# Decayed attention ahead of two MLPs: the carried states as one scan per unit, chunk innermost, with four input slots and a smaller descriptor scratch

## The chip, the cores and the metric

One core of a Trainium2 chip runs the whole program. Its engines are TensorE (PE, with weight loads shown apart as PEld), VectorE (DVE), ScalarE (ACT), GpSimd (POOL) and SyncE (SP, whose queue issues the transfers). The metric is the device time of one execution in microseconds (us); lower is better.

## The reference

```python
batch, n_heads, seq, head_dim = (4, 8, 576, 64)
scores = scale * np.matmul(q, k.transpose(0, 1, 3, 2))
gamma = 1.0 - 2.0 ** (-5.0 - np.arange(H, dtype=np.float32))
rel = pos[:, None] - pos[None, :]
Dmat = np.where(rel >= 0, gamma[:, None, None] ** rel[None, :, :], 0.0)
ret = scores * Dmat[None, :, :, :]
attn_out = np.matmul(ret, v)
...
x = np.ascontiguousarray(attn_out.transpose(0, 2, 1, 3)).reshape(B * S, H * D)
h = np.maximum(x @ w_in, 0.0)        # 2304 x 512 by 512 x 2048
x = h * h @ w_out
a = x @ w_a                          # 2304 x 512 by 512 x 1536
b = x @ w_b
return (a * b @ w_out).astype(np.float32)
```

Attention has no softmax: a score is multiplied by a power of its head's decay. The sum over earlier tokens can therefore be carried from chunk to chunk as a state of 64 x 64 values per head.

## The kernel before, in words

**Attention.** The 576 tokens of a sequence are cut into 9 chunks of 64 (`C = 64`). Two heads make a pair, one head on partitions 0 to 63 and the other on 64 to 127. For each of the 4 sequences there are 5 units: one for each pair with its first 7 chunks (`LONG = 7`; `first` is 0), and one with the last 2 chunks of all four pairs. A unit loads its q and k into a slot of `qkr` and its v and k into a slot of `vr` (both rings of 3 slots). ScalarE scales a copy of v into `tv` (line 613). TensorE then makes three groups of 64x64 products in full fp32: the scores, the states (`tv` against k, a new contribution per chunk) and, one unit later, the sums (masked scores against v, and carried states against q). VectorE masks the scores into `pt` (line 700), carries the states in `carry_states` (lines 721 and 722) and scales the sums into the activations `xt` (line 685). The carry is one copy for the first chunk and then one fused multiply and add per chunk, out = before x decay + new, on 64 columns each. The carried states lie in `sa`, chunk after chunk; the last one of a pair goes to `sp`, from where the unit of the last chunks takes it up.

**MLPs.** Weights arrive as 64-bit words in `wraw` (and, early on, in a part of `xt` that is still free); ScalarE and VectorE turn each tile of 128x512 into fp32 (lines 369 to 399) and split it into a high and a low part (lines 240 and 243, tile `w`). The activations are split the same way into `xb`. `up` and `down` are the first MLP's two products for the chunks of `FIRST`; the rest of the program follows later and reads its weights back from memory (`kept`, `parts`).

**Order.** All work is first recorded as steps with costs per engine, then `Plan.order` writes one order for each engine by due times and modelled costs. Each engine runs its rows strictly in that order. Attention's units are put between the MLP's chunks at a rate (`RATE`), after the first sequence's units have been placed ahead of everything. All large transfers stand in one queue, SP's, and a transfer into a slot waits there until the slot's last reader is done.

Of the kernel before, what the change touches and what calls it, by code (L numbers as in the profile page):

```python
# [11 lines left out]
F32 = mybir.dt.float32  # L12
# [5 lines left out]
ALU = mybir.AluOpType  # L18
PSUM = bass.MemoryType.PSUM

B, H, S, D = 4, 8, 576, 64
NT, DM, F1, F2 = 2304, 512, 2048, 1536
P = 128
NP = H // 2
# [3 lines left out]
LONG = 7  # L28
# [22 lines left out]

WF, WL, WE, RAWS = 4, 4, 2, 2
SLOTS = dict(
    g=2, r=2, gh=2, qkr=3, vr=3, tv=2, pt=2, sa=2, wraw=4, ys=4,
)

POOL_SLACK, POOL_BIAS = 1e9, 1e6
# [159 lines left out]
def tile_retention_two_mlps(  # L217
# [10 lines left out]
    nc = tc.nc  # L228
    eng = {"ACT": nc.scalar, "DVE": nc.vector, "POOL": nc.gpsimd}
    V, A, G, T = nc.vector, nc.scalar, nc.gpsimd, nc.tensor  # L230
    plan = Plan()

    def mm(o, l, r, start, stop):
        T.matmul(o, l, r, start=start, stop=stop, skip_group_check=True)  # L234
# [30 lines left out]
    def ring(pool_, tag, shape, dtype, n):  # L265
        rings[tag] = [[pool_.tile(shape, dtype, name=f"{tag}{i}") for i in range(n)], 0]

    def slot(tag):
        r = rings[tag]
        i = r[1] % len(r[0])  # L270
        r[1] += 1
        plan.renew((tag, i))
        return r[0][i], (tag, i)
# [12 lines left out]
    st = ExitStack()  # L286
    ap = st.enter_context(tc.tile_pool(name="attn", bufs=1, side="right"))
# [2 lines left out]
    ring(ap, "vr", [P, 2 * LONG * D], F32, SLOTS["vr"])  # L290
    ring(ap, "tv", [P, LONG * D], F32, SLOTS["tv"])
    ring(ap, "pt", [P, most * C], F32, SLOTS["pt"])
    ring(ap, "sa", [P, (LONG - 1) * D], F32, SLOTS["sa"])

    ring(ap, "ys", [P, 512], F32, SLOTS["ys"])
    ring(ap, "wraw", [P, 1024], U32, SLOTS["wraw"])
    vt = ap.tile([P, 3 * NP], F32, name="vt")
    gt = ap.tile([P, NP, C], F32, name="gt")
# [5 lines left out]
    mask = ap.tile([P, C], F32, name="mask")  # L304
    md = ap.tile([P, NP, C], F32, name="md")
    sp = [ap.tile([P, D], F32, name=f"sp{p}") for p in range(NP)]

    V.memset(mask, 1.0)
    first = ap.tile([P, 2], F32, name="first")
# [225 lines left out]
    def attention():  # L535
        turn = [0]

        def banks(b):

            sets = [(4, 5, 6)] if b else [(4, 5, 6), (0, 1, 2)]  # L540
            turn[0] += 1
            return [(bank[i], ("bank", i)) for i in sets[turn[0] % len(sets)]]

        for h in half:
# [3 lines left out]
                lambda _, h=h: G.affine_select(  # L548
                    out=mask[h], in_=mask[h], pattern=[[1, C]], compare_op=ALU.is_ge, fill=zero,
                    base=0, channel_multiplier=-1,  # L550
                ),
# [3 lines left out]
        def decays(p):  # L555
            plan.add(
                {"DVE": 230},
                lambda e: V.tensor_scalar(
                    out=md[:, p], in0=mask, scalar1=vt[:, p:p + 1], scalar2=None, op0=ALU.mult
                ),  # L560
                [("mask",), ("vt",)], [("md", p)],
            )

        class Unit:

# [12 lines left out]
            def load(self):  # L578
# [24 lines left out]
                if b == 0 and self.p is not None:  # L603
                    decays(self.p)
# [14 lines left out]
        def cell(i, n=C):  # L619
            return slice(i * n, i * n + n)  # L620

        def products(new, old):

            b = (new or old).b
            (s, ks), (st, kst), (x, kx) = banks(b)
            scores, states, sums = [], [], []

            if new:  # L630
                n = len(new.cells)
                for i in range(n):
                    for h in half:
                        scores.append((s[h, cell(i)], new.r[h, cell(n + i)], new.r[h, cell(i)], i == 0))
                for i in range(len(new.leave)):
                    for h in half:
                        states.append((st[h, cell(i)], new.v[h, cell(n + i)], new.tv[h, cell(i)], i == 0))
            if old:
                for i in range(len(old.cells)):
                    for k, h in enumerate(half):  # L640
                        sums.append((x[half[1 - k], cell(i)], old.v[h, cell(i)], old.pt[h, cell(i)], i == 0))
                for i, (q, j) in enumerate(old.cells):
                    if j:
                        for k, h in enumerate(half):
                            sums.append((x[half[1 - k], cell(i)], old.state[q, j][h], old.r[h, cell(i)], False))

            def f(gs):
                for k in range(0, max(map(len, gs)), 2):
                    for g in gs:
                        for o, l, r, first in g[k:k + 2]:  # L650
                            mm(o, l, r, first, True)

            def run(keys, *gs):
                rd = [k for r, _ in keys for k in r]
                wr = [w for _, w in keys]
                plan.add({"PE": 58 * max(map(len, gs)) + 330}, lambda e: f(gs), rd, wr)

            ksc, kstt = ([new.kr], ks) if new else None, ([new.kv, new.kt], kst) if new else None
            ksu = ([old.kr, old.kv, old.kp] + old.kstate, kx) if old else None

            if b and new and old:
                run([ksc, kstt, ksu], scores + states, sums)
            else:
                if new:
                    run([ksc], scores)
                if old:
                    run([ksu], sums)
                if new:
                    run([kstt], states)
            if old:  # L670
                weigh(old, x, kx)
            if new:
                mask_scores(new, s, ks)
                carry_states(new, st, kst)

        def weigh(u, x, kx):

            np_, per = len(u.pairs), u.last - u.first
            c0 = u.b * S + u.first * C
            x = x[:, :np_ * per * C].rearrange("p (q c n) -> p q c n", q=np_, n=C)  # L680
            ps = slice(u.pairs[0], u.pairs[-1] + 1)
            n = per * C
            plan.add(
                {"DVE": 1.042 * np_ * n + 145},
                lambda e: V.tensor_tensor(
                    out=xt[:, ps, c0:c0 + n].rearrange("p q (c n) -> p q c n", n=C),
                    in0=x,
                    in1=gt[:, ps].unsqueeze(2).to_broadcast([P, np_, per, C]), op=ALU.mult,
                ),
                [("gt",), kx], [w for q in u.pairs for w in tokens("xt", q, c0, n)],  # L690
                [m for k in lenders for m in plan.users.get(k, ())] if c0 + n > LENT else (),
            )

        def mask_scores(u, s, ks):
            np_, per, n = len(u.pairs), u.last - u.first, len(u.cells)
            ps = slice(u.pairs[0], u.pairs[-1] + 1)
            u.pt, u.kp = slot("pt")
            plan.add(
                {"DVE": 1.042 * n * C + 145},
                lambda e: V.tensor_tensor(  # L700
                    out=u.pt[:, :n * C].rearrange("p (q c n) -> p q c n", q=np_, n=C),
                    in0=s[:, :n * C].rearrange("p (q c n) -> p q c n", q=np_, n=C),
                    in1=md[:, ps].unsqueeze(2).to_broadcast([P, np_, per, C]), op=ALU.mult,
                ),
                [ks] + [("md", q) for q in u.pairs], [u.kp],
            )

        def carry_states(u, st, kst):

            sa, ksa = slot("sa")  # L710
            u.state = {(q, LONG): sp[q] for q in u.pairs}
            u.kstate = [ksa] + ([("sp", q) for q in u.pairs] if u.first else [])
            for i, (q, j) in enumerate(u.leave):
                o, ko = (sp[q], ("sp", q)) if j + 1 == LONG else (sa[:, cell(i, D)], ksa)
                u.state[q, j + 1] = o
                before, kb = u.state.get((q, j)), [ksa, ("sp", q)]
                far = vt[:, 2 * NP + q:2 * NP + q + 1]

                def carry(e, o=o, i=i, before=before, far=far):
                    if before is None:  # L720
                        return V.tensor_copy(o, st[:, cell(i, D)])
                    return V.scalar_tensor_tensor(
                        out=o, in0=before, scalar=far, in1=st[:, cell(i, D)], op0=ALU.mult, op1=ALU.add
                    )

                rd = [kst, ("vt",)]
                if before is not None:
                    rd.append(("sp", q) if j == LONG else ksa)
                plan.add({"DVE": 270 if j else 222}, carry, rd, [ko])
# [3 lines left out]
        for n, (b, p) in enumerate(units):  # L733
            new = Unit(b, p)
# [156 lines left out]
    xo = []  # L891
    tmp = []

    rings_a = ["qkr", "vr", "tv", "pt", "wraw", "vt", "gt", "mask", "md", "sp", "sa", "ys"]

    def mlps():
        prev = None
# [10 lines left out]
    def rest():  # L908
# [430 lines left out]
        for _ in downs:  # L1339
            pass  # L1340

    att = attention()
    while env["done"] < READY[0]:
        next(att)
# [86 lines left out]
```

## Time and profile before

| what | value |
|---|---|
| time, median of 3 runs | 854.11 us (851.86 to 855.42) |
| the profiled execution's own time | 854.09 us |
| its span, first to last instruction | 852.4 us |
| TensorE busy | 834.8 us (98%), 6540 matmuls |
| VectorE busy | 731.9 us (86%) |
| ScalarE busy | 565.9 us (66%) |
| mean granted TensorE clock | 0.998 of full speed |

A busy share is a mean over the program; what the change can move is read from the stretch in which attention runs. The trace shows each fp32 64x64 product as two matmul instructions, so its counts for attention are twice those of the program's order.

### The profile page before, as it was taken

The page shows a single profiled execution, that of the slowest core. Times are in us where ns is not written, and L with a number is a line of the kernel's source. Part 1 is how long each engine was busy: PE and PEld are TensorE (multiplying, and loading weights), DVE is VectorE, ACT ScalarE, POOL GpSimd, SP SyncE. Part 2 cuts the span into 40 slices and gives each one's busy share as a digit, 9 for nine tenths or more (in the row PEclk, how much of TensorE's full clock was granted, in tenths as well). Part 3 has the DMA queues.
Part 4 walks back from the last instruction along what each step waited for, and adds up shares of the span by engine and source line. Part 5 has one row for each costly group of instructions (what it writes and reads, how often), then busy time and mean ns, then how long its engine had stood idle before and what let it go on. Part 6 is the DMA issues. An engine that isn't in the chain of part 4 may idle for free.

```text
span 852.4 us, 17685 instructions
## 1 busy us (share of the span) xinstructions
PE 834.8 (98%) x6540; PEld 801.4 (94%) x6540; DVE 731.9 (86%) x1531; ACT 565.9 (66%) x1180; POOL 0.7 (0%) x6
## 2 busy tenths in 40 slices
PE   5899999999999999999999999999999999999998
PEld 5788888889999999999999999999999999999997
DVE  5999874878799999999899989999786789888885
ACT  4676562767888877978796565676556576556560
POOL 0000000000000000000000000000000000000000
PEclk9999999999999999999999999999999999999999
DMA  9865861379877668757847888755554455655432
GB/s 322 296 238 187 290 217 62 113 251 301 264 249 236 210 216 257 229 190 242 294 151 237 286 294 285 222 172 171 160 187 145 142 164 163 184 175 163 138 90 75
DMA packets 89734, 176.15 MB, mean 207 GB/s; under 512 B 9904, under 2 KB 34864, under 8 KB 89648
## 3 DMA queue, kind: packets, MB, share of 16 engines
q1 hardware_dynamic: 89504, 175.02, 63.7%
q8 instruction: 51, 0.84, 0.4%
q14 instruction: 35, 0.29, 0.1%
q10 hardware_dynamic: 144, 0.01, 0.0%
HBM read 134.75 MB, written 40.24 MB: 205 GB/s over the span
## 4 chain that ended last, share of the span: by engine, by line
PE 86%; DMA 6%; DVE 4%; ACT 3%; issue 1%; SPq 0%; ACTq 0%; DVEq 0%
PE bank L234 86%; DMA w<-kept 2%; DMA raw<-w 2%; DMA wraw<-w 1%; ACT w L240 1%; DMA vr<-vk 1%; DVE w L243 1%; DVE xt L246 1%; DMA vt<-vtab 0%; DVE wf L388 0%; ACT tv L613 0%; ACT xb L240 0%; DVE wf L399 0%; ACT wf L369 0%; ACT bank L240 0%
## 5 line engine op out<-in xcount | busy, mean ns | idle before, releaser
L234 PE MATMUL bank<-xo,w 128*128 128x384 f32 x1838 | 389.5, 335 | 0.9 <-ACT bank L240 0.7
L234 PEld LDWEIGHTS bank<-xo,w 128*128 128x128 f32 x1838 | 324.3, 188 | 3.1 <-ACT bank L240 2.4
L234 PE MATMUL bank<-xb,w 128*128 128x384 f32 (+2 forms) x1044 | 229.1, 347 | 1.1 <-ACT r L824 0.8
L240 ACT CAST w<-w 128x512 fp32r<-128x512 f32 (+1 forms) x316 | 156.6, 519 | 86.2 <-DMA w<-kept 69.4
L234 PEld LDWEIGHTS bank<-xb,w 128*128 128x128 f32 x1044 | 184.1, 188 | 13.3 <-ACT r L824 1.2
L243 DVE TENSOR_TENSOR w<-w 128x512 fp32r<-128x512 f32 (+1 forms) x316 | 170.9, 560 | 20.8 <-ACT w L240 19.1
L234 PE MATMUL bank<-gh,w 128*128 128x384 f32 (+2 forms) x750 | 171.9, 352 | 0.2
L234 PEld LDWEIGHTS bank<-gh,w 128*128 128x128 f32 x750 | 131.9, 188 | 12.4 <-DVE w L243 0.5
L234 PE MATMUL bank<-w,w 128*128 128x384 f32 x546 | 123.9, 334 | 0.1
L234 PEld LDWEIGHTS bank<-w,w 128*128 128x128 f32 x546 | 97.1, 188 | 0.5 <-DVE xt L246 0.4
L246 DVE TENSOR_TENSOR xt<-bank,xt 128x384 f32<-128x384 f32 x128 | 69.7, 552 | 8.4 <-PE bank L234 7.9
L240 ACT COPY bank<-bank 128x384 f32<-128x384 f32 x122 | 57.2, 469 | 16.5 <-PE bank L234 13.9
L234 PE MATMUL bank<-ghl,w 128*128 128x384 f32 x186 | 40.9, 334 | 0.0
L243 DVE TENSOR_TENSOR xo<-xt,xo 128x768 fp32r<-128x768 f32 x36 | 33.6, 951 | 1.9 <-ACT xo L240 1.9
L395 ACT ACTIVATE we<-raw 128x512 int32<-128x512 uint32 x48 | 31.9, 668 | 3.1 <-DVE wf L399 1.5
L240 ACT CAST xo<-xt 128x768 fp32r<-128x768 f32 x36 | 29.1, 831 | 6.0 <-issue 5.4
L234 PEld LDWEIGHTS bank<-ghl,w 128*128 128x128 f32 x186 | 33.0, 188 | 0.0
L243 DVE TENSOR_TENSOR gh<-g,gh 128x512 fp32r<-128x512 f32 (+2 forms) x40 | 24.5, 614 | 8.1 <-ACT g L827 6.8
L399 DVE CUSTOM_DVE_ANT_0 wf<-wf,we 128x1024 uint16<-128x1024 uint16 x45 | 30.7, 685 | 0.4
L613 ACT ACTIVATE tv<-vr,vt 128x448 f32<-128x448 f32 (+1 forms) x32 | 15.0, 500 | 21.5 <-DMA vr<-vk 19.7
L824 ACT ACTIVATE r<-bank 128x512 f32<-128x512 f32 (+1 forms) x30 | 16.5, 551 | 19.1 <-PE bank L234 18.9
L234 PE MATMUL bank<-tv,vr 64*64 64x64 f32 x512 | 20.5, 233 | 8.6 <-ACT tv L613 8.6
(241 smaller groups left out, 962.2 us busy)
## 6 DMA issues: line engine op xcount, KB each, us to landing
w<-kept SPq DMA_DIRECT2D x167, 256.0 KB, 3.7
raw<-w SPq DMA_DIRECT2D x48, 512.0 KB, 4.7
w<-kept SPq DMA_DIRECT2D x149, 128.0 KB, 3.0
kept<-wf SPq DMA_DIRECT2D x49, 256.0 KB, 4.2
w<-parts SPq DMA_DIRECT2D x24, 512.0 KB, 3.5
kept<-wl SPq DMA_DIRECT2D x36, 256.0 KB, 4.9
wraw<-w SPq DMA_DIRECT2D x16, 512.0 KB, 7.3
vr<-vk SPq DMA_DIRECT2D x16, 448.0 KB, 5.3
```

What stands on the lines that cost most here:

```text
L234: T.matmul(o, l, r, start=start, stop=stop, skip_group_check=True)
L240: return lambda e: A.copy(o(), i()) if e == "ACT" else eng[e].tensor_copy(o(), i())
L243: return lambda e: eng[e].tensor_sub(o(), a(), b())
L246: return lambda e: eng[e].tensor_add(o(), a(), b())
L395: lambda e: A.activation(like(rest), lo(), AF.Copy, scale=LO_ULPS), [kraw], [ke],
L399: lambda e: V._custom_dve(ADD32_U16LIMBS, out=w().bitcast(U16), in0=w().bitcast(U16), in1=rest.bitcast(U16)),
L613: lambda e, to=to, ti=ti, q=q: A.activation(self.tv[:, to], self.v[:, ti], AF.Copy, scale=vt[:, NP + q:NP + q + 1]),
L824: lambda e, o=o: A.activation(r[:, :n], o[:, :n], AF.Relu), [ko], [kr],
```

## The change

Carrying the seven chunks of a full unit is now one VectorE scan over 448 columns. For that the states of a unit are written with the chunk innermost: chunk i of the state goes to columns i, i + 7, i + 14 and so on of its PSUM bank. Along a row the scan computes value = factor x previous + new, and the factor tile `fade` holds the pair's decay everywhere but in each seventh column, where it is 0 and so starts anew. `fade` is set up by two memsets and one multiplication per pair. The carried states are then read by TensorE at a stride of 7 elements, and the last one is copied to `sp` by ScalarE. The units of the last chunks keep the old form. `qkr` and `vr` have 4 slots in place of 3, `sa` one more chunk, and the program's scratch for dynamic descriptors is set to 1024.

```diff
 SLOTS = dict(
-    g=2, r=2, gh=2, qkr=3, vr=3, tv=2, pt=2, sa=2, wraw=4, ys=4,
+    g=2, r=2, gh=2, qkr=4, vr=4, tv=2, pt=2, sa=2, wraw=4, ys=4,
 )
...
-    ring(ap, "sa", [P, (LONG - 1) * D], F32, SLOTS["sa"])
+    ring(ap, "sa", [P, LONG * D], F32, SLOTS["sa"])
...
+    fade = ap.tile([P, NP, D * LONG], F32, name="fade")
+    V.memset(fade, 1.0)
+    V.memset(fade[:, :, ::LONG], 0.0)
 
     V.memset(mask, 1.0)
...
+            plan.add(
+                {"DVE": 440},
+                lambda e: V.tensor_scalar(
+                    out=fade[:, p], in0=fade[:, p],
+                    scalar1=vt[:, 2 * NP + p:2 * NP + p + 1], scalar2=None, op0=ALU.mult,
+                ),
+                [("vt",)], [("fade", p)],
+            )
...
-                        states.append((st[h, cell(i)], new.v[h, cell(n + i)], new.tv[h, cell(i)], i == 0))
+                        to = st[h, cell(i)] if new.first else st[h, i:LONG * D:LONG]
+                        states.append((to, new.v[h, cell(n + i)], new.tv[h, cell(i)], i == 0))
...
             sa, ksa = slot("sa")
+            if not u.first:
+                q = u.p
+                u.kstate = [ksa]
+                u.state = {(q, j): sa[:, j - 1::LONG] for j in range(1, LONG)}
+                plan.add(
+                    {"DVE": 1090},
+                    lambda e: V.tensor_tensor_scan(
+                        out=sa, data0=fade[:, q], data1=st[:, :LONG * D], initial=0.0, op0=ALU.mult, op1=ALU.add
+                    ),
+                    [kst, ("fade", q)], [ksa],
+                )
+                plan.add({"ACT": 250}, lambda e: A.copy(sp[q], sa[:, LONG - 1::LONG]), [ksa], [("sp", q)])
+                return
...
-    nc = bacc.Bacc("TRN2", target_bir_lowering=False, num_devices=1)
+    nc = bacc.Bacc("TRN2", target_bir_lowering=False, num_devices=1, dynamic_dma_scratch_size=1024)
```

The rows of the orders below are the engines' own, with buffer numbers.

VectorE, the first three units of the first sequence. Before, with `sa_117` and `sa_118` the carried states and `bank_66` and `bank_70` the banks of the new ones:

```order
L558 TENSOR_SCALAR md<-mask,vt 128x64 x4
L721 COPY sa_117<-bank_66 128x64
L722 SCALAR_TENSOR_TENSOR sa_117<-sa_117,vt,bank_66 128x64 x5
L700 TENSOR_TENSOR pt_115<-bank_65,md 128x448
L722 SCALAR_TENSOR_TENSOR sp_131<-sa_117,vt,bank_66 128x64
L721 COPY sa_118<-bank_70 128x64
L722 SCALAR_TENSOR_TENSOR sa_118<-sa_118,vt,bank_70 128x64 x2
L700 TENSOR_TENSOR pt_116<-bank_69,md 128x448
L722 SCALAR_TENSOR_TENSOR sa_118<-sa_118,vt,bank_70 128x64 x3
L685 TENSOR_TENSOR xt<-bank_71,gt 128x448
```

The same place now (L729 is the scan, which the list prints under the name of its family; L568 makes the factors):

```order
L568 TENSOR_SCALAR fade<-fade,vt 128x448
L561 TENSOR_SCALAR md<-mask,vt 128x64
L712 TENSOR_TENSOR pt_117<-bank_65,md 128x448
L729 SCALAR_TENSOR_TENSOR sa_119<-fade,bank_66 128x448
L712 TENSOR_TENSOR pt_118<-bank_69,md 128x448
L697 TENSOR_TENSOR xt<-bank_71,gt 128x448
L729 SCALAR_TENSOR_TENSOR sa_120<-fade,bank_70 128x448
```

Seven carries have become one scan, the mask stands ahead of it, and the first unit's `xt` stands ahead of the second unit's scan. The first two of these rows occur four times in turn, once per pair.

SP's queue, from the seventh load on. Before, after six loads of the first three units:

```order
L252 DMA gt<-gtab 128x256
L252 DMA wraw_123<-w 128x1024
L252 DMA wraw_125<-w 128x1024
L252 DMA wraw_124<-w 128x1024
L252 DMA qkr_107<-qk 128x896
L252 DMA vr_110<-vk 128x896
L252 DMA vr_111<-vk 128x768
L252 DMA qkr_108<-qk 128x1024
L252 DMA xt<-w 128x2x512
```

Now, from the same place:

```order
L252 DMA qkr_110<-qk 128x896
L252 DMA gt<-gtab 128x256
L252 DMA vr_114<-vk 128x896
L252 DMA wraw_125<-w 128x1024
L252 DMA vr_111<-vk 128x768
L252 DMA qkr_107<-qk 128x1024
L252 DMA wraw_127<-w 128x1024
L252 DMA qkr_108<-qk 128x896
L252 DMA vr_112<-vk 128x896
```

The fourth unit's loads now have slots of their own and stand ahead of the first weights, and two of the first three weight loads have moved behind loads of attention.

VectorE at the split of the first block of activations (`xb`), with the masks and products just ahead. Before:

```order
L685 TENSOR_TENSOR xt<-bank_71,gt 128x4x128
L399 ISA wf_74<-wf_74,we_78 128x1024
L380 TENSOR_SCALAR wf_73<-wf_73 128x512
L700 TENSOR_TENSOR pt_116<-bank_69,md 128x448
L243 TENSOR_TENSOR xb_79<-xt,xb_79 128x512 x2
L243 TENSOR_TENSOR xb_80<-xt,xb_80 128x512 x2
L721 COPY sa_118<-bank_70 128x64
```

Now:

```order
L697 TENSOR_TENSOR xt<-bank_71,gt 128x4x128
L391 SCALAR_TENSOR_TENSOR wf_74<-wraw_126,wf_74 128x512
L729 SCALAR_TENSOR_TENSOR sa_120<-fade,bank_70 128x448
L243 TENSOR_TENSOR xb_79<-xt,xb_79 128x512 x2
L243 TENSOR_TENSOR xb_80<-xt,xb_80 128x512 x2
```

The scan of the sixth unit (the first of the second sequence) has moved ahead of the split; before, that unit's carry began behind it.

From TensorE's 515th row of before on, in the last part of attention, the orders of TensorE agree row by row to the end of the program, apart from buffer and line numbers.

## Rows read from the trace of the kernel before

**Rows 1.** The page: busy time, share of the span and instructions of two engines.
```profile
PE 834.8 (98%) x6540; PEld 801.4 (94%) x6540; DVE 731.9 (86%) x1531; ACT 565.9 (66%) x1180; POOL 0.7 (0%) x6
```

**Rows 2.** Windows: engine busy in each stretch (instructions), granted clock, DMA share, GB/s.
```profile
10.00:15.00 5.00, 3.45 (x136) 3.31 (x131) 3.99 (x12) 2.14 (x4) 0.00 (x0) 1.00 1.01 365
15.00:20.00 5.00, 2.93 (x90) 2.65 (x91) 4.52 (x13) 3.88 (x9) 0.00 (x0) 0.99 0.91 320
20.00:25.00 5.00, 5.00 (x144) 5.00 (x142) 4.22 (x16) 2.50 (x7) 0.00 (x0) 0.67 0.96 293
25.00:30.00 5.00, 3.82 (x129) 3.55 (x124) 4.93 (x12) 1.22 (x2) 0.00 (x0) 1.00 0.90 292
30.00:35.00 5.00, 3.99 (x40) 3.07 (x40) 4.34 (x10) 4.71 (x9) 0.00 (x0) 1.00 1.00 385
35.00:40.00 5.00, 4.23 (x18) 3.30 (x18) 5.00 (x14) 4.67 (x10) 0.00 (x0) 1.00 0.80 299
40.00:160.00 120.00, 119.87 (x1970) 98.80 (x1970) 94.48 (x230) 70.89 (x128) 0.00 (x0) 1.00 0.57 188
160.00:846.00 686.00, 684.56 (x3931) 675.14 (x3930) 605.02 (x1213) 473.08 (x1013) 0.00 (x0) 1.00 0.64 204
```

**Rows 3.** Timeline of TensorE: start, duration, instructions, idle before them and its releaser.
```profile
5.23 1.76 PE L234 MATMUL bank<-tv,vr 64*64 64x64 f32 x28 [5.23 <-ACT tv L613]
...
31.97 3.03 PE L234 MATMUL bank<-xb,w 128*128 128x512 f32 x12
```

**Rows 4.** The chain that ended last, in order of time, around 30 us.
```profile
23.92 6.28 DMA vr<-vk
...
30.29 0.67 ACT tv L613
```

**Rows 5.** Transfers of the first 40 us: packets, bytes, mean rate.
```profile
DMA packets 4406, 12.78 MB, mean 320 GB/s; under 512 B 575, under 2 KB 703, under 8 KB 4400
```

**Rows 6.** Timeline of VectorE, the start.
```profile
0.88 0.11 DVE L308 MEMSET mask<- 128x64 f32 x1 [0.88 <-PEq L1419]
0.94 0.06 DVE L310 MEMSET first<- 128x2 f32 x1
4.62 0.74 DVE L558 TENSOR_SCALAR md<-mask,vt 128x64 f32<-128x64 f32 x4 [3.62 <-DMA vt<-vtab]
```

**Rows 7.** Groups by line and shape, 0 to 150 us: busy us, mean ns, idle before.
```profile
L722 DVE SCALAR_TENSOR_TENSOR sa<-sa,vt,bank 128x64 f32<-128x64 f32 x80 | 22.0, 275 | 0.6
...
L234 PE MATMUL bank<-tv,vr 64*64 64x64 f32 x512 | 20.5, 233 | 8.6 <-ACT tv L613 8.6
...
L234 PE MATMUL bank<-qkr,sa 64*64 64x64 f32 x448 | 19.0, 223 | 2.0 <-issue 2.0
...
...
L369 ACT ACTIVATE wf<-wraw 128x512 f32<-128x512 f32 x16 | 10.5, 669 | 7.0 <-DVE w L243 3.8 <-DMA wraw<-w 3.2
L700 DVE TENSOR_TENSOR pt<-bank,md 128x448 f32<-128x448 f32 x16 | 9.9, 618 | 0.0
...
L373 DVE TENSOR_SCALAR wf<-wf 128x512 f32<-128x512 f32 x20 | 8.4, 420 | 1.3 <-ACT wf L369 1.3
...
L240 ACT CAST w<-wf 128x512 fp32r<-128x512 f32 x12 | 7.4, 617 | 5.3 <-DVE wf L399 5.2
...
L613 ACT ACTIVATE tv<-vr,vt 128x64 f32<-128x64 f32 x16 | 4.4, 336 | 4.3 <-DMA vr<-vk 4.3
...
L721 DVE COPY sa<-bank 128x64 f32<-128x64 f32 x16 | 3.5, 222 | 10.7 <-PE bank L234 10.7
L700 DVE TENSOR_TENSOR pt<-bank,md 128x512 f32<-128x512 f32 x4 | 2.7, 684 | 0.0
```

**Rows 8.** Timeline of TensorE inside a unit of the second sequence.
```profile
40.20 0.23 PE L234 MATMUL bank<-qkr 64*64 64x64 f32 x2
...
40.96 0.22 PE L234 MATMUL bank<-tv,vr 64*64 64x64 f32 x2
```

More of the change, by code (lines that the diff above doesn't have):

```diff
@@ L710, in carry_states @@
             sa, ksa = slot("sa")
+            if not u.first:
[11 more added lines that the diff above has]
+                return
             u.state = {(q, LONG): sp[q] for q in u.pairs}
-            u.kstate = [ksa] + ([("sp", q) for q in u.pairs] if u.first else [])
+            u.kstate = [ksa] + [("sp", q) for q in u.pairs]
             for i, (q, j) in enumerate(u.leave):
@@ L892, in tile_retention_two_mlps @@
     tmp = []
-    rings_a = ["qkr", "vr", "tv", "pt", "wraw", "vt", "gt", "mask", "md", "sp", "sa", "ys"]
+    rings_a = ["qkr", "vr", "tv", "pt", "wraw", "vt", "gt", "mask", "md", "fade", "sp", "sa", "ys"]
     def mlps():
```

## The prediction

> **What bounds the kernel now.** I read the windows first [rows 2]. From 160 to 846 us TensorE is idle for 686.00 - 684.56 = 1.4 us, and from 40 to 160 us for 0.13 us, although attention goes on there until about 150 us. VectorE is busy for 94.48 of those 120 us, but TensorE does not wait for it. Over the whole span TensorE is busy 98% [rows 1]. So after 40 us only one thing can move the end: how long TensorE's own instructions take. Before 40 us it is otherwise. The six windows from 10 to 40 us leave TensorE idle for 1.55, 2.07, 0, 1.18, 1.01 and 0.77 us, 6.6 us in all; it issues its first product at 5.23 us, and its first MLP product at 31.97 us [rows 3]. In the same windows the DMA share is 0.80 to 1.01 [rows 2]: the transfers are full nearly all the time. The granted clock is 0.67 from 20 to 25 us, after TensorE had sat idle for 3.6 us of the ten before. [...] The chain shows what opens the MLP: a `vr` load that is issued at 23.92 us, its ScalarE copy at 30.29 us [rows 4], and behind that copy, in ScalarE's order, the split of the first block into `xb`.
>
> TensorE's order is the same from the end of attention on, and TensorE never waits there to speak of. Hence whatever time the change wins or loses up to about 150 us arrives at the end unchanged. The sum is made against the profiled execution, 854.09 us (span 852.4 and 1.7 around it), which is the median of 854.11.
>
> **The transfers at the start.** With three slots the queue held 20 loads up to and with the `vr` load of [rows 4]: counted from the queue's order, 9024 KB or 9.24 MB. That load is for the seventh unit, the second of the second sequence. With four slots it is the 18th: fewer weights and no load of the eighth unit stand ahead of it, 8000 KB or 8.19 MB. The 1.05 MB less, at the 290 to 320 GB/s of the windows between 15 and 30 us [rows 2] and of the first 40 us as a whole [rows 5], is 3.3 to 3.6 us. By the transfers alone the MLP would begin 3.4 us sooner. Below that the gain could be nothing, if the loads only change places and another one is late instead.
>
> **VectorE up to the MLP.** A unit's carry now costs one copy of 222 ns and six multiply-adds of 275 ns, 1.87 us [rows 7]. The trace has no scan. From below I bound it by an ordinary product of 448 columns out of PSUM, 618 ns. From above: 64 more columns cost 684 - 618 = 66 ns, so 448 columns cost 0.46 us of the 0.62; a scan that needs two steps per column takes 0.62 + 0.46 = 1.08 us. I take 1.08, since each value needs the one before it. A unit then saves 0.79 us, 16 units 12.6 us, of which all that lies after 40 us is off the path [rows 2]. Up to the split of the first block VectorE had four such carries and now has five scans, since the sixth unit's scan has moved ahead: 4 x 1.87 - 5 x 1.08 = 2.1 us less. It was also idle for 1.01, 0.48, 0.78 and 0.07 us between 10 and 30 us [rows 2], 2.3 us that earlier loads could fill. So VectorE lets the split come 2.1 to 4.4 us sooner, and the transfers 3.4. I take 3.1, nearly the middle of the first and below the second.
>
> [...]
>
> **Setting up the factors.** Two memsets of 64 and 2 columns take 0.11 and 0.06 us [rows 6], 0.8 ns a column. The 1792 columns of `fade` are then 1.5 us and the 256 strided ones 0.3 to 0.5 us. They push the mask's memset from 0.88 to about 3 us, and GpSimd's cut of the mask behind it. Cover: the masks wait for `vt` in any case, until 4.62 us [rows 6]. If that cover were gone, up to 1 us. The four multiplications are at most 0.42 us each by the 512-column row of [rows 7], 1.5 us among the masks, so the masks end at about 6.9 us in place of 5.4. That delays only the first `pt`, whose scores need the first `qkr` and then TensorE for some 1.8 us, as its first group of 28 did [rows 3]. Taken at 0.
>
> **ScalarE.** It gains 16 copies to `sp`. The nearest row, 64 columns, is 336 ns [rows 7], so at most 5.4 us on an engine that is busy 66% [rows 1]. Each waits for a scan, and the `tv` copy of a later unit is queued behind it: the first stands ahead of the third unit's `tv`, which has to wait for the sixth load of the queue in any case. Taken at 0.
>
> **TensorE's strided operands.** This is the open price, and it would fall on the bound engine. The states of full units are written at a stride of 7 elements and read back as weights at that stride. The trace has 512 state products and 448 with `sa` [rows 7]; of these 448 and 384 belong to full units. Products go in steps of 58 ns, two side by side, and in the later sequences four, 13 of them from 40.20 to 40.96 us [rows 8]. The first sequence's steps lie in the stretch where TensorE waits anyway. In the other three there are 12 full units with 14 steps each for states, 168, and the strided reads mostly share them; only the fourth pair's `sa` is read beside the next unit, whose states are not strided, 12 for each of 3 sequences: 204 steps. Bounds: nothing, if both go at the speed of now; or each step doubled, 204 x 58 ns = 11.8 us. A gain is excluded, for the same elements move. The nearest row is a strided read by another engine: ScalarE takes 669 ns for 512 values at a stride of 2, and 617 ns for 512 side by side [rows 7], 8% more, which on these steps is 0.9 us. Since a step may hold slack that covers this (the load of weights runs beside the products), I take 0 and keep both ends.
>
> [...]
>
> **The smaller scratch.** GpSimd runs 6 instructions in 0.7 us [rows 1], two of them on the mask and four constants, and all large loads are SP's, so nothing uses it: 0, but for the room that it gives the slots.
>
> **Sum.** 854.1 - 3.1 = 851.0 us.
>
> **The rivals.**
> *The front closes further.* Beside the transfers' 3.4 us, TensorE may lose the waits that follow the MLP's first product, 1.0 us of the 1.01 + 0.77 idle from 30 to 40 us [rows 2], because VectorE is then ahead with the weights; and it may keep the full clock, 1.65 us. 854.1 - 6.0 = 848.1 us. For it: the chain runs through loads and VectorE, and both get less to do. Against: the transfers stay full, so gaps remain and the clock may fall again.
> *Strides cost a matmul time.* From 36 ns a step on (7.4 us over 204 steps, against the 3.1 won) the change is slower by over 0.5%; at 58 ns it ends at 854.1 - 3.1 + 11.8 = 862.8 us. For it: the slower engine is the bound one, without cover after 40 us. [...]
> *Strides cost some.* At 15 to 30 ns a step, 3.1 to 6.1 us, the front's gain is eaten: 854 to 857 us.
> *The change doesn't reach the start.* If another load or VectorE holds the split where it was, the time stays at 854.1 us, for VectorE's saving lies under TensorE after 40 us.
>
> **How the numbers follow.** No change can be told from one under 0.5%, 4.3 us. The forecast (851.0, with 849.5 to 853 as its own range, that is a start won by 1.1 to 4.6 us): 0.42. Front closes further, 846.5 to 849.5: 0.22. Some stride price or no gain, 853 to 858.4: 0.20. Strides dear, above that: 0.16. Faster needs less than 849.8 us: all of the second case and a tenth of the first, 0.26. Slower is above 858.4: 0.16. The range from 847.5 to 858.5 leaves out about 0.05 below and 0.15 above.
>
> **What would show it.** In the profile after: the first `xb` product at about 29 us; scans near 1.1 us; steps of 58 ns in the units of the second sequence, or longer ones if strides cost; TensorE idle between 10 and 40 us of about 3.5 us in place of 6.6; after 40 us none. The forecast is wrong if the steps grow, or if the first `xb` product stays near 32 us.

## The result, and the profile after

The change made the kernel slower: 862.28 us (median of 6 runs, 860.23 to 863.98) against 854.62 us (6 runs beside them), a ratio of 1.0091 with a 95% interval of 1.0065 to 1.0117. The forecast was 851.0 us with a range up to 858.5, so the time lies outside the range, on the slower side. The profiled execution of the changed kernel took 860.23 us (span 858.5), 6.1 us more than that of before. It is the fastest of the six and the only one with a mean granted clock of 1.0 (the others have 0.994 to 0.999), so its profile shows a start that is better than usual.

The page of the changed kernel, to be held against [rows 1]: TensorE is busy 8.1 us more with the same 6540 matmuls, so its instructions take longer; VectorE runs 88 instructions fewer.

```profile
PE 842.9 (98%) x6540; PEld 810.1 (94%) x6540; DVE 732.0 (85%) x1443; ACT 569.7 (66%) x1194; POOL 0.7 (0%) x6
```

The windows of the changed kernel, as in [rows 2], and one more pair, cut at 218 us, well behind the end of attention:

```profile
10.00:15.00 5.00, 3.98 (x128) 3.85 (x126) 3.46 (x5) 1.65 (x3) 0.00 (x0) 1.00 1.03 402
15.00:20.00 5.00, 5.00 (x144) 5.00 (x146) 3.36 (x8) 2.64 (x8) 0.00 (x0) 1.00 0.71 225
20.00:25.00 5.00, 3.95 (x118) 3.81 (x114) 4.78 (x11) 3.20 (x7) 0.00 (x0) 1.00 0.99 337
25.00:30.00 5.00, 3.38 (x123) 3.24 (x123) 4.06 (x9) 3.51 (x7) 0.00 (x0) 1.00 1.01 385
30.00:35.00 5.00, 3.44 (x18) 2.21 (x21) 5.00 (x9) 3.95 (x9) 0.00 (x0) 1.00 1.05 410
35.00:40.00 5.00, 5.00 (x120) 4.43 (x121) 5.00 (x11) 4.50 (x9) 0.00 (x0) 1.00 0.98 375
40.00:160.00 120.00, 120.00 (x1841) 100.04 (x1840) 85.80 (x158) 67.25 (x129) 0.00 (x0) 1.00 0.55 176
...
40.00:218.00 178.00, 177.27 (x2151) 149.41 (x2150) 135.61 (x250) 108.12 (x208) 0.00 (x0) 1.00 0.60 190
218.00:853.00 635.00, 633.77 (x3653) 631.54 (x3652) 562.61 (x1128) 438.99 (x943) 0.00 (x0) 1.00 0.63 201
```

The kernel before, cut 7 us sooner:

```profile
40.00:211.00 171.00, 170.76 (x2254) 143.17 (x2254) 137.95 (x314) 105.90 (x199) 0.00 (x0) 1.00 0.63 205
211.00:846.00 635.00, 633.67 (x3648) 630.77 (x3647) 561.55 (x1128) 438.07 (x943) 0.00 (x0) 1.00 0.63 201
```

From 10 to 40 us TensorE is idle for 5.25 us in place of 6.6, and from 40 to 160 us it does not wait at all. The stretch from 218 to 853 us is as long as 211 to 846 us was before, and TensorE is busy there for 633.77 us against 633.67. All the loss lies ahead of it, in the stretch with attention: from 40 us on it takes 7 us longer, although it holds 103 matmuls fewer, since more of attention now stands ahead of 40 us.

The groups of the changed kernel (0 to 160 us, as in [rows 7]) name the instruction:

```profile
L234 PE MATMUL bank<-qkr,sa 64*64 64x64 f32 x448 | 29.7, 269 | 1.5 <-issue 1.5
L234 PEld LDWEIGHTS bank<-qkr,sa 64*64 64x64 f32 x448 | 27.5, 198 | 1.7 <-issue 1.7
L234 PE MATMUL bank<-tv,vr 64*64 64x64 f32 x512 | 22.0, 230 | 0.2 <-ACT tv L624 0.2
L729 DVE TENSOR_TENSOR_SCAN sa<-fade,bank 128x448 f32<-128x448 f32 x16 | 17.3, 1083 | 11.8 <-PE bank L234 11.8
L734 ACT COPY sp<-sa 128x64 f32<-128x64 f32 x16 | 5.0, 311 | 11.5 <-DVE sa L729 11.4
L568 DVE TENSOR_SCALAR fade<-fade,vt 128x448 f32<-128x448 f32 x4 | 1.8, 447 | 1.4 <-DMA vt<-vtab 1.4
L308 DVE MEMSET fade<- 128x1792 f32 x1 | 1.6, 1552 | 1.2 <-PEq L1444 1.2
```

The products with `sa` as weights went from 223 to 269 ns, and their weight loads are 198 ns. The state products, whose outputs are now strided, stayed at 230 ns (233 before). The scan is 1.083 us.

TensorE's timeline: its first product and its first `xb` product, to be held against [rows 3], and the inside of the first unit of the second sequence, as in [rows 8]:

```profile
4.54 1.76 PE L234 MATMUL bank<-qkr 64*64 64x64 f32 x28 [4.54 <-DMA qkr<-qk]
...
30.08 0.73 PE L234 MATMUL bank<-xb,w 128*128 128x512 f32 x2 [1.24 <-ACT xb L240]
...
35.63 0.23 PE L234 MATMUL bank<-qkr 64*64 64x64 f32 x2
...
35.69 0.23 PE L234 MATMUL bank<-qkr 64*64 64x64 f32 x2
...
35.76 0.28 PE L234 MATMUL bank<-qkr,sa 64*64 64x64 f32 x2
...
35.88 0.28 PE L234 MATMUL bank<-qkr,sa 64*64 64x64 f32 x2
...
36.00 0.28 PE L234 MATMUL bank<-qkr,sa 64*64 64x64 f32 x2
```

Steps with scores still come some 58 ns apart (35.63, 35.69). Steps that read a carried state come every 116 to 120 ns. Of the 448 matmuls with `sa` 384 belong to the 16 full units, and two make a step: 384 / 16 / 2 = 12 such steps a unit, so it takes 0.7 us longer; in the 12 full units behind the first sequence that is 144 x 58 ns = 8.4 us on an engine that never waits.

### The profile page after: what moved, and what is told of

The parts are those of the page before. It is cut to its first block, busy times and chain, and to the rows that moved or that the text cites. A ratio compares the mean times of both kernels' runs of the same rounds, so it can differ in the third digit from the quotient of the medians.

```text
span 858.5 us, 17616 instructions
## 1 busy us (share of the span) xinstructions
PE 842.9 (98%) x6540; PEld 810.1 (94%) x6540; DVE 732.0 (85%) x1443; ACT 569.7 (66%) x1194; POOL 0.7 (0%) x6
## 3 DMA queue, kind: packets, MB, share of 16 engines
q1 hardware_dynamic: 89504, 175.02, 63.1%
## 4 chain that ended last, share of the span: by engine, by line
PE 90%; DMA 4%; DVE 3%; issue 1%; ACT 1%; SPq 0%; DVEq 0%; ACTq 0%
PE bank L234 90%; DMA raw<-w 2%; DMA w<-kept 2%; DMA vr<-vk 1%; DVE xb L243 0%; DVE xt L246 0%; DVE wf L383 0%; DVE gh L243 0%; DVE wf L391 0%; DVE wf L402 0%; DVE wf L376 0%; ACT wf L372 0%; DVE wl L391 0%; DVE xt L697 0%; ACT w L240 0%
## 5 line engine op out<-in xcount | busy, mean ns | idle before, releaser
L234 PE MATMUL bank<-qkr,sa 64*64 64x64 f32 x448 | 29.7, 269 | 1.5 <-issue 1.5
L234 PEld LDWEIGHTS bank<-qkr 64*64 64x64 f32 x576 | 19.8, 143 | 10.2 <-DMA qkr<-qk 4.5
```

## The experiments

All ratios are to the kernel before, run on the same chip, with 95% intervals.

### One half of the layout at a time

The kernel before, with its copies and multiply-adds as they were; only where the carried states lie is changed (the tile `sa` is one chunk longer for it):

```diff
+        def place(sa, i):
+            return sa[:, i:i + 7 * D - i:7]
...
-                o, ko = (sp[q], ("sp", q)) if j + 1 == LONG else (sa[:, cell(i, D)], ksa)
+                o, ko = (sp[q], ("sp", q)) if j + 1 == LONG else (place(sa, i) if not u.first else sa[:, cell(i, D)], ksa)
```

> The kernel before with one edit: the carried states of a full unit lie chunk innermost in their tile, so TensorE reads them as weights at a stride of 7 elements; states, carry, slots and order stay as before. If the strided weight reads are the cost: steps with carried states go from 58 to about 116 ns, 144 of them in the last three sequences, 8.4 us, and the time is 862 to 864 us. If the stride of the states in PSUM, the scan or the new order is the cost: no change, 854 to 855 us.

Measured: 862.65 us, 1.0097 [1.0081, 1.0114]. Its groups (0 to 160 us):

```profile
L234 PE MATMUL bank<-qkr,sa 64*64 64x64 f32 x448 | 29.9, 271 | 1.6 <-issue 1.6
L234 PEld LDWEIGHTS bank<-qkr,sa 64*64 64x64 f32 x448 | 27.7, 198 | 1.9 <-issue 1.9
L726 DVE SCALAR_TENSOR_TENSOR sa<-sa,vt,bank 128x64 f32<-128x64 f32 x80 | 27.1, 339 | 0.6
```

The strided weights alone, without scan, slots or strided outputs, bring the whole loss: 0.97% of 853.82 is 8.3 us, against 8.4 by the steps. VectorE's carries are slower here too (339 ns), but TensorE is idle for only some 0.1 us from 40 to 160 us (0.13 before), so it does not wait for them. The other half, strided outputs in PSUM alone:

```diff
-                        states.append((st[h, cell(i)], new.v[h, cell(n + i)], new.tv[h, cell(i)], i == 0))
+                        to = st[h, cell(i)] if new.first else st[h, i:LONG * D:LONG]
+                        states.append((to, new.v[h, cell(n + i)], new.tv[h, cell(i)], i == 0))
...
-                        return V.tensor_copy(o, st[:, cell(i, D)])
+                        return V.tensor_copy(o, new_state)
```

> The kernel before with one edit: the states of a full unit are written to PSUM with the chunk innermost, at a stride of 7 elements, and the old carry reads them from there; the carried states lie side by side. If strided writes of products cost nothing, as the steps without carried states in the changed kernel suggest: 854 to 855 us. [...]

Measured: 854.44 us, 1.0009 [0.9993, 1.0026]; its state products take 232 ns, against 233 side by side [rows 7]. For these fp32 outputs at a stride of 28 bytes no price can be measured.

### From which stride on

The kernel before with the carried states interleaved in groups of S, so that TensorE reads them at a stride of S elements; these three runs also have a longer `sa` and the smaller scratch of the changed kernel:

```diff
+        def place(sa, i):
+            o = i // S * S * D + i % S
+            return sa[:, o:o + S * D - i % S:S]
```

> The kernel before with the carried states of full units interleaved in twos, so that TensorE reads weights at a stride of 2 elements (8 bytes); smaller scratch, all else as before. If any stride halves the weight read: steps of 116 ns, about 862 us. If it is the distance that counts, one value per 16-byte line being slow and two not: steps of 58 ns, 854 to 855 us.

> The same with the states interleaved in fours, a stride of 16 bytes. If one value per 16-byte line is what is slow: steps of 116 ns as at a stride of 7, 862 to 863 us. If the price grows with the distance: between 58 and 116 ns.

> The kernel before, with the carried states of full units interleaved in threes, so that TensorE reads them as weights at a stride of 12 bytes; all else as in the run at a stride of 4 elements. If what counts is how many runs of 16 bytes a row of weights touches, 64 values at 12 bytes touch 48 of them and at 8 bytes 32: the weight load should then lie between 137 and 200 ns, near 170, and the time between 854 and 862 us, near 858. If the price begins as soon as two neighbouring values no longer come in one such run in pairs, it is the full one: 198 to 200 ns and 861 to 863 us. If 12 bytes is as cheap as 8, 137 ns and 854 us.

Measured: at a stride of 2 elements 853.89 us, 0.9999 [0.9983, 1.0015], so that the smaller scratch costs nothing either; at 3, 857.12 us, 1.0031 [1.0016, 1.0046]; at 4, 861.76 us, 1.0083 [1.0054, 1.0113]. The rows of the tile `sa` from 40 to 150 us, where the last-chunk units are few, give TensorE's weight loads with minimum, median and maximum in ns. In the kernel before, side by side, all three are 135. At a stride of 2:

```profile
L234 PEld LDWEIGHTS bank<-qkr,sa x330: 134/135/139, 41.6 to 150.0; 64*64 64x64 f32 x165
```

At 3:

```profile
L234 PEld LDWEIGHTS bank<-qkr,sa x320: 135/171/175, 40.6 to 144.9; 64*64 64x64 f32 x160
```

At 4:

```profile
L234 PEld LDWEIGHTS bank<-qkr,sa x312: 135/213/213, 41.4 to 150.0; 64*64 64x64 f32 x156
```

At 7 (the run on the kernel before above):

```profile
L234 PEld LDWEIGHTS bank<-qkr,sa x302: 135/209/213, 42.2 to 149.9; 64*64 64x64 f32 x151
```

64 fp32 values touch 32, 48, 64 and 64 runs of 16 bytes at these strides; the load takes 135, 171, 213 and 209 ns. At these four the load follows the number of runs and not the distance: 16 and 28 bytes cost nearly the same (213 and 209 ns). A stride of 2 puts two values in each run, 4 and 7 put one, and 3 lies between, in the trace (135, 213 and 209, 171 ns) as in the count. The middle case came out at 171 ns, as the first of its expectations said. Its time rose by 2.6 us (1.4 to 3.9), where 144 steps that are 30 ns longer (8 steps from 49.02 to 49.72 us are 88 ns each) make 4.3; the difference is not explained.

### The slots, and the scan with weights side by side

The changed kernel, with six carried states of each unit copied side by side by ScalarE ahead of their use (`sd`, two slots):

```diff
+                sd, ksd = slot("sd")
+                u.kstate = [ksd]
+                u.state = {(q, j): sd[:, cell(j - 1, D)] for j in range(1, LONG)}
...
+                    lambda e: A.copy(sd.rearrange("p (j d) -> p j d", d=D),
+                        sa.rearrange("p (d j) -> p j d", j=LONG)[:, :LONG - 1]),
```

> The changed kernel with one step more: after each scan ScalarE copies the first six carried states to a tile in which each chunk lies side by side, and TensorE reads its weights there. If the strided weight reads are the cost: steps back at 58 ns, 8.4 us less after 40 us and up to 2.8 us less before, 851 to 854 us. If another part of the change costs (order, slots, strided states): stays near 862 us.

Measured: 855.91 us, 1.0020 [1.0007, 1.0034]. In the two runs below that also have this copy it takes 925 and 931 ns (means of 16), and the products with carried states are back at 219 and 220 ns. The price is gone, but the gain at the start is not there. The same with three slots:

> The changed kernel with carried states copied side by side by ScalarE, and 3 slots: the scan alone. If the scan frees VectorE at the start: 850 to 853 us, below both kernels. If the loads, not VectorE, hold the start: 853 to 855 us. If four slots were what helped: 856 us or more.

853.35 us, 0.9993 [0.9975, 1.0011]: the scan, with dense weights, gives nothing that can be measured, and no kernel of the study beats the one before. A scan that writes the states side by side itself was not tried. The changed kernel with three slots:

> The changed kernel with 3 slots for qkr and vr as before; scan, strides and scratch as changed. If the strided weight reads are the whole loss and the slots are worth nothing: 862 to 863 us. If the four slots lose at the start because the first weights are loaded later: below 861 us. If they win: above 864 us.

864.05 us, 1.0116 [1.0093, 1.0138]. By its expectation that is a win of the fourth slot, but the interval overlaps that of the changed kernel (1.0065 to 1.0117), and no other pair of runs shows such a win. And the kernel before with only the four slots and the smaller scratch:

```diff
-    g=2, r=2, gh=2, qkr=3, vr=3, tv=2, pt=2, sa=2, wraw=4, ys=4,
+    g=2, r=2, gh=2, qkr=4, vr=4, tv=2, pt=2, sa=2, wraw=4, ys=4,
...
-    nc = bacc.Bacc("TRN2", target_bir_lowering=False, num_devices=1)
+    nc = bacc.Bacc("TRN2", target_bir_lowering=False, num_devices=1, dynamic_dma_scratch_size=1024)
```

> The kernel before with the slots and the scratch alone: qkr and vr with 4 slots, scratch for descriptors 1024; the carry as before. If the slots open the MLP sooner: 1 to 4 us less, 851 to 853.5 us. If VectorE, not the loads, holds the start: 854 to 855 us. If the scratch or the order of loads costs: above 856 us.

855.42 us, 1.0012 [0.9999, 1.0025]: no gain. Its timelines, of an execution that took 858.83 us, the slowest of its twelve, show what the fourth slot moves: the first weights now come after attention's loads, VectorE's row on them stands ahead of the carries, and TensorE has a long wait of its own. VectorE, then ScalarE, then TensorE:

```profile
20.70 0.43 DVE L373 TENSOR_SCALAR wf<-wf 128x512 f32<-128x512 f32 x1 [2.32 <-ACT wf L369]
```
```profile
20.01 0.66 ACT L369 ACTIVATE wf<-wraw 128x512 f32<-128x512 f32 x1 [3.89 <-DMA wraw<-w]
```
```profile
22.30 0.69 PE L234 MATMUL bank<-pt,vr 64*64 64x64 f32 x7 [4.34 <-issue]
```

I took the late weights for the cause of both waits. Two runs set the due time of the first four weight loads 12 us earlier, on the kernel with the copy and on the changed kernel:

```diff
-            late[i] = min(t, default=self.pe)
+            late[i] = min(t, default=self.pe) - self.early.get(i, 0.0)
...
+        state_["raws"] = state_.get("raws", 0) + 1
+        if state_["raws"] <= 4:
+            plan.early[load] = 12000
```

> The kernel with the scan, four slots and the copy to side by side (855.9 us when timed), but the due time of the first four weight loads set 12 us earlier, so that the first three stand as the 5th, 8th and 10th load of SP's queue in place of the 12th, 13th and 16th. Theory A (the front's gain is lost because four slots push the first weights behind attention's loads, and VectorE and SP's queue then stand behind them): the first weights land some 5 us sooner, TensorE is idle between 10 and 40 us for clearly less than the 5.8 us of that kernel, and the time falls to 852.5 to 854 us. Theory B (the front is held by something else, the transfers as a whole or VectorE's and ScalarE's work): the time stays at 855.5 to 856.5 us, whatever the first weights do.

> The changed kernel itself, with the first four weight loads set 12 us earlier in due time (the first three are the 4th, 7th and 10th load of SP's queue). By theory A the time falls by 2 to 3 us from the changed kernel's 862.3, to 859.5 to 860.5, since the weight reads still cost 58 ns a step after the first sequence (8.4 us) and only the front is mended. By theory B it stays at 861.5 to 863 us.

Measured: 853.90 us, 1.0009 [0.9993, 1.0025], and 862.97 us, 1.0107 [1.0086, 1.0128]. The first time is as theory A had it, but its interval overlaps that of the copy without it, and TensorE is idle from 10 to 40 us for 5.6 us, which is not clearly less than 5.8; the second time is against A. Late weights alone don't explain it.

### The change without its price

To see the front by itself, the changed kernel reads its weights side by side out of the interleaved tile; the order on every engine is that of the changed kernel. Its sums then take from earlier chunks values that belong to no one state, and only its time is read.

```diff
-                u.state = {(q, j): sa[:, j - 1::LONG] for j in range(1, LONG)}
+                u.state = {(q, j): sa[:, cell(j - 1, D)] for j in range(1, LONG)}
```

> The changed kernel in its own order of instructions, but TensorE reads 64 values side by side out of the carried states where the changed kernel reads every seventh; the values are then not those of one state, so what the sums add for earlier chunks is left out of the comparison and only the time is read. It is the change without the price of its weight reads and without any copy in its place. The prediction's sum as it stood: 851.0 us, since the price was its only failed term. Rival: the front gains nothing, whatever the weight reads cost, and the time is that of the kernel before, 854 us. If the weight reads explain everything but cost less or more than 144 steps of 58 ns, the changed kernel's 862.3 less 8.4 is 853.9 us; with the 48 steps of the first sequence on the path as well, 851.1 us.

> The same with three slots: the scan alone, without a price on its reads and without a copy. If VectorE's saving ahead of the first split (2.1 us by the rows) reaches the end, 852 us; if the loads hold the split, 854 us. Beside the run with four slots it shows what the fourth slot does: 851 against 852 to 854 if it opens the MLP sooner, 854 to 856 against 852 if it only pushes the weights back.

> The same with four slots and the first four weight loads 12 us earlier in due time (4th, 7th and 10th load of SP's queue). If late first weights are what holds the front, 2 to 3 us below the run with four slots as it is; if not, the same within 1 us, or above it, since attention's loads are then later.

Measured: 855.05 us, 1.0007 [0.9985, 1.0029]; 855.57 us, 1.0014 [0.9995, 1.0032]; 856.70 us, 1.0021 [1.0000, 1.0041]. A gain of 3.1 us would be 0.9964, outside the first interval, which leaves room for 1.3 us at most: the front won nothing that can be measured, with either number of slots, and earlier weights did not help. The single executions of the first kernel spread from 849.52 to 857.50 us, those of the kernel before beside it from 850.11 to 859.09. TensorE's timeline of the first of these kernels, in an execution of 856.30 us, shows where time goes:

```profile
14.74 0.97 PE L234 MATMUL bank<-pt,vr 64*64 64x64 f32 x25 [1.61 <-issue]
...
19.29 0.33 PE L234 MATMUL bank<-qkr,sa 64*64 64x64 f32 x2 [0.84 <-issue]
...
28.85 0.37 PE L234 MATMUL bank<-qkr,sa 64*64 64x64 f32 x2 [5.72 <-issue]
...
35.04 0.73 PE L234 MATMUL bank<-xb,w 128*128 128x512 f32 x2 [0.90 <-ACT xb L240]
```

The first three of these waits, 8.2 us, are released by nothing in the profile ("issue"). In the changed kernel the same order waits 1.01 and 1.51 us at two of these three places, and the kernel before has 1.63 and 0.38 us of such waits. The windows of the same execution:

```profile
20.00:25.00 5.00, 3.13 (x113) 2.99 (x108) 4.49 (x11) 1.97 (x4) 0.00 (x0) 1.00 0.91 300
25.00:30.00 5.00, 1.15 (x26) 1.15 (x28) 0.63 (x2) 1.87 (x3) 0.00 (x0) 0.64 1.00 389
30.00:35.00 5.00, 4.14 (x104) 4.00 (x102) 3.56 (x8) 2.40 (x5) 0.00 (x0) 0.68 0.93 288
35.00:40.00 5.00, 4.17 (x10) 3.05 (x11) 5.00 (x9) 3.54 (x7) 0.00 (x0) 0.66 0.94 341
```

The longest wait costs more than its own length: the granted clock was 1.00 up to 25 us; with TensorE idle for 5.72 us, until 28.85 us, it fell to 0.64 and was 0.68 and 0.66 from 30 to 40 us. By estimate, 5 us at 0.68 and 5 us at 0.66 are at most 1.6 + 1.7 = 3.3 us of work lost. Over all executions the mean granted clock is 0.9958 in this kernel and 0.9973 in the kernel before beside it, by estimate some 1.2 us of 855.

### What these waits are

Summing the counts of TensorE's timeline up to such a wait gives, from its first matmul, 222 and 477 in the kernel before and in the changed one, 222, 350 and 477 in the kernel above, and in every other kernel up to here one or more of these numbers, give or take one, and no other, whatever the order of its work: 128 apart. A matmul has a weight load beside it (6540 of each in [rows 1]), so this is 256 instructions. To part the count from the work, I put products of zeros ahead of everything, which shifts the work against the count:

```diff
+    idle = ap.tile([P, C], F32, name="idle")
+    V.memset(idle, 0.0)
+    for i in range(32):
+        h = slice(64 * (i % 2), 64 * (i % 2) + 64)
+        mm(bank[7][h, :C], idle[h], idle[h], True, True)
```

> The kernel before, with 32 products of zeros put ahead of TensorE's first work, in a bank that is overwritten later; each is two matmuls and two weight loads, 64 matmuls in all. Theory C: TensorE's waits in the front that nothing in the profile releases are waits for its own instructions, which come in blocks of 256 (128 matmuls with their weight loads) through the same transfers as the data. They then stand at fixed counts of TensorE's own instructions, 222, 350 or 477 matmuls from its start, and with 64 more at the start they come 64 matmuls earlier in the work: after 158, 286 and 413 of the program's own. Theory D: they belong to the work, to data that the trace does not name; they then stay before the same products, after 286, 414 and 541 matmuls counted from the start. The time stays within 1% of before in both.

> The same with 16 products, 32 matmuls. Theory C: such waits again only after 222, 350 and 477 matmuls from the start, that is 32 matmuls earlier in the work than before. Theory D: after 254, 382 and 509. The time stays within 1% of before in both.

> The changed kernel with four slots and its carried states read side by side (the values are those of no one state, so what earlier chunks add is left out of the comparison), with 32 products of zeros ahead, as in the run on the kernel before. Theory C: the waits that nothing releases stand after 222, 350 and 477 matmuls from the start, not after 286, 414 and 541. Where a block's transfer comes late the wait is long (5.7 us in the run without the products), so the time may move by up to 3 us to either side of that run's 855.

Measured: 853.83 us, 1.0009 [0.9996, 1.0022]; 855.50 us, 1.0023 [1.0005, 1.0041]; 856.47 us, 1.0046 [1.0029, 1.0063]. The last one's timeline of TensorE, with its 64 extra matmuls in the first row:

```profile
3.55 3.68 PE L234 MATMUL bank<-idle 64*64 64x64 f32 x64 [3.55 <-DVE idle L315]
13.61 0.39 PE L234 MATMUL bank<-tv,vr 64*64 64x64 f32 x6 [1.83 <-issue]
19.41 0.50 PE L234 MATMUL bank<-qkr 64*64 64x64 f32 x9 [0.63 <-issue]
24.79 0.50 PE L234 MATMUL bank<-qkr 64*64 64x64 f32 x10 [1.73 <-issue]
31.26 0.27 PE L234 MATMUL bank<-qkr,sp 64*64 64x64 f32 x2 [2.99 <-issue]
```

These four waits stand after 222, 350, 477 and 605 matmuls, extra ones included, and so before other products of the work than without them. In the kernel before with 64 ahead they stand after 477 and 605 (1.48 and 0.45 us), with 32 ahead after 222 and 477 (1.17 and 1.31 us). The places follow the count and not the work, as theory C says, and D falls. That TensorE waits for its own instructions there is C's reading of these counts.

## Why the prediction was wrong

**The step that failed: "TensorE's strided operands ... I take 0 and keep both ends."** The price was real and fell on the bound engine: 58 ns a step, the upper end. Of the two strided operands only one pays, the weights (loads of 209 ns in place of 135); the 168 steps counted for the states' writes cost nothing by themselves (232 ns a product against 233), and the right count behind the first sequence is the 144 steps with `sa` of full units, 8.4 us and not 11.8. Measured, it is 8.3 us alone (the kernel before with strided weights), 7.2 us inside the change (1.0091 against 1.0007) and 8.7 us inside it with three slots (1.0116 against 1.0014), the last two uncertain by some 3 us. The error was in choosing the nearest row: a ScalarE read at 8 bytes, 8% slower (669 against 617 ns, on two different operations [rows 7]), said nothing on TensorE at 28 bytes, and at 8 bytes TensorE's loads took 135 ns, as side by side. The hope that a step holds slack for a longer load failed: a load that is 36 ns longer (12 bytes) makes the step 30 ns longer, and one that is 74 to 78 ns longer (28 and 16 bytes) makes it 58 to 62 ns longer.

**The start, -3.1 us: not there.** This is the second step that failed: "I take 3.1" made the time at which the first split opens the gain at the end. The scan came out as worked out, and part of the forecast start did too: the changed kernel's first `xb` product stands at 30.08 us, 1.9 us sooner than in [rows 3], TensorE is idle for 1.3 us less from 10 to 40 us (3.1 were forecast), and the granted clock does not fall (1.00 in all six windows). But the transfers that bound the chain of [rows 4] gave way to something else. The changed kernel's chain, in order of time:

```profile
13.90 1.01 issue
...
23.95 1.51 issue
25.46 0.46 PE bank L234 x5
25.94 0.62 DVE xt L697
...
29.97 1.00 DVE sa L729
30.97 2.39 DVE xb L243 x4
...
34.89 136.42 PE bank L234 x1822
```

Two waits that nothing releases (1.01 and 1.51 us) now stand on the chain, and behind the second one VectorE is busy nearly without a break from 25.94 to 34.89 us, with rows on weights and with the sixth unit's scan ahead of the split. In the kernel without the price all 8.2 us of such waits are on the chain. The first sequence's strided reads lie in the front too; their 48 steps, 2.8 us, were taken as covered by waits, and the 8.3 us of strided weights alone do not speak against that. Without the price the gain still doesn't come (1.0007), nor by the scan alone (0.9993 and 1.0014) or the slots alone (1.0012). So the bound of the front was not one chain of loads. How much of the 3.1 us VectorE, the order of the weights, these waits and the clock behind them each ate is not settled: a profile is one execution, and the waits differ much between two with the same order (2.5 us in the changed kernel's profile, 8.2 in the one without the price).

**The rivals.** "Strides cost a matmul time" gave 862.8 us and the run 862.28, but by two errors that cancel: 3.1 us won that were not, and 3.4 us too many paid. Its mechanism is the one that happened, on the reads. "The change doesn't reach the start" is also what happened to the other half; the two were held apart as rivals where they belong together, 854.1 + 8.4 = 862.5 us. "The front closes further" counts 1.65 us for the clock, which is 0.33 of the 5 us at 0.67 in [rows 2]; that they come back at the end no run shows: in the changed kernel's profile the clock was 1.00 from 10 to 40 us, and the execution took 6.1 us longer.

**What was right.** The scan is 1.083 us where 1.08 was taken. The factors' memset is 1.55 us and each multiplication 447 ns, and TensorE's first product did not come later (4.54 us against 5.23). ScalarE's copies to `sp` are 311 ns, and none stands on the chain that ended last. After 40 us TensorE hardly waits, so what its own instructions take longer there arrives at the end.

## What to carry to other kernels

Before a layout is changed for one engine's sake, look at how the bound engine reads it: at the strides that were run, an fp32 weight read by TensorE stayed cheap as long as every run of 16 bytes gave it two values (135 ns a load, 209 and 213 with one), and a price on one product is to be multiplied by all products of that kind. Where TensorE waits on nothing that the profile names while the transfers are full, count its instructions up to the wait: here the counts repeated (222, 350, 477, 605 matmuls), and by theory C it was the program itself that came late. And a wait that is shortened at a start with three engines and a full queue is no gain until a run without the other parts of the change shows it at the end.

## What the runs showed of the hardware

- **Weight loads.** 64 fp32 columns: 135 ns with the values side by side or 8 bytes apart, 171 at 12, 213 at 16 and 209 at 28 bytes. The step of two products goes from 58 to 88 and to 116 to 120 ns.
- **Strided outputs in PSUM.** 64 fp32 values 28 bytes apart: 230 to 232 ns a product, 233 side by side.
- **Other engines at 28 bytes.** VectorE's multiply-add on 64 columns, reading and writing `sa`, goes from 275 to 339 ns.
- **TensorE's instructions.** Waits that nothing releases stand after 222, 350, 477 and 605 matmuls, 128 apart, also with 64 more matmuls ahead; by theory C TensorE's instructions arrive in blocks of 256. The page of the changed kernel lists a queue that it calls instruction, with packets, MB and its share of the 16 engines, of which the queue with the data has 63.1%:

```profile
q8 instruction: 51, 0.84, 0.4%
```

By estimate, 0.84 MB in 51 packets is some 16 KB each, 64 bytes for each of 256 instructions, and over 13,080 matmuls and weight loads it is 64 bytes for one as well; that this queue carries TensorE's instructions is read from this agreement. TensorE waited up to 5.72 us at such a place, while the DMA share was 0.91 to 1.00 (the kernel without the price, 20 to 30 us). That the full transfers make the block late is argued from this; no run took the transfers away. Of such waits 2.0 us show in the profile of the kernel before (1.63 and 0.38), 2.5 in the changed kernel's (1.01 and 1.51), 8.2 in that of the kernel without the price (1.61, 0.84 and 5.72).
